# Scores of the first two head pairs as full fp32 products, with nine products on a constant ahead of them

## The chip, the cores and the metric

The kernel runs on one core of a Trainium2 chip. The metric is the device time of one execution in microseconds (us); lower is better. TensorE (PE) has two clock levels that matter here, 1.2 and 2.4 GHz; the profile gives the clock that was granted as a share of the full one.

## The reference, cut to what matters

A soft-capped attention is followed by two feed-forward stages. Only the attention is touched by the change:

```python
def _attn_ref(q, k, v, cap):               # q, k, v: (4, 12, 448, 64)
    scale = 1.0 / np.sqrt(q.shape[-1])
    scores = scale * np.matmul(q, k.transpose(0, 1, 3, 2))
    scores = cap * np.tanh(scores / cap)
    scores = scores - np.max(scores, axis=-1, keepdims=True)
    attn = np.exp(scores)
    attn = attn / (np.sum(attn, axis=-1, keepdims=True) + 1e-09)
    return np.matmul(attn, v).astype(np.float32)
# then, on the result reshaped to x (1792, 768):
#   r = relu(x @ w_in); x = (s * r * r + b) @ w_out      (d_ff = 2048)
#   soft mixture over 8 experts of 4 slots, with phi, w1, w2
```

`q` and `k` are drawn at standard deviation 6.4, so the scores are large. `w_in` and `w_out` arrive as float64.

## The kernel before, in words

**Pairs.** The 48 heads are taken as 24 pairs `p`, two heads on the two halves of the 128 partitions (64 each). Two pairs make a quad `Q`, 12 in all. For a pair, qT is 128 x 448 and kT 128 x 512: three full chunks of 128 keys, and a fourth in which the last 64 keys of both heads lie together.

**Loads.** `load_qk` issues the two loads of a pair on the SP queue. Pairs 0 and 1 go straight into the tiles `tmp` and `hh` (`c["early"]`, line 903), which lie idle at the start; later pairs into one buffer each of `q2` and `k2`, so that pair p + 1 can be loaded only when pair p has been split.

**Splitting.** `prep_pair` splits q and k into a high part, rounded to the reduced format fp32r, and the rest (`split`, lines 77 to 79): a cast (line 78) and a subtraction on DVE (line 79). The cast is on DVE for p < 6 except pair 1, whose casts are on ACT. The four results have three buffers each.

**Scores.** `scores` (line 114) makes one chunk of one pair: kh·qh + kh·ql + kl·qh, three reduced products for each of the two heads, on the two halves of the rows (line 125); the fourth chunk takes both heads in one product (line 122). Pairs of even number write their scores into one PSUM tile, the others into another. ACT then takes the tanh (lines 129, 131) and, when both pairs of a quad have a chunk, the exponential (line 194) of 4 x 448 columns.

**What runs beside it.** Products of the exponentials with v (line 229) and with a constant of ones (lines 212, 214) are full fp32 products on PE, 32 columns wide, four of them side by side. DVE adds the exponentials up (line 201) and takes the reciprocal (line 218). `attention` is a generator; `run` takes 52 steps of it (a little over three quads) before the feed-forward starts, and at every sixth step one unit of `convert`: it loads a slice of float64 `w_in` or `w_out` (line 351, 768 KB, two buffers), scales it on ACT (line 356) and puts the bits together on DVE (lines 361, 383, 387). `down` and `fold` (lines 435 to 448) reduce a w_out slice with `phi`, through `tmp` and `pw`, which is a part of `hh`. The result of quads 0 and 1 also goes through `hh` (line 241).

**What sets the order.** Everything before the branch on `cap` (line 939) is laid out as one block and everything inside as another. Within a block the tile framework's planner fixes each engine's order from the order of the program and from estimated durations; `high_priority` moves a few instructions ahead. At run time each engine takes its list strictly in order. The loads of pairs 0 and 1 and the constants stand before the branch, all else behind it.

**Behind the opening** come four feed-forward blocks (`hidden`, line 497; products at line 509) with the rest of the attention woven in, then a tail that streams the expert weights.

Of the kernel before, what the change touches and what calls it, by code (L numbers as in the profile page):

```python
# [7 lines left out]
F32 = mybir.dt.float32  # L8
# [6 lines left out]
PSUM = bass.MemoryType.PSUM  # L15
DRAM = bass.MemoryType.DRAM

P = 128
B, H, S, D = 4, 12, 448, 64
NP = H // 2  # L20
# [13 lines left out]
KF = S // P  # L34
# [5 lines left out]
STEPS = 8  # L40
LAST = 3
CASTS = NP
LEAD = 10
WIDE = 6
VISITS = (4, 7, 10, 13)
# [7 lines left out]
def load_qk(nc, io, p, q2, k2):  # L53

    nc.sync.dma_start(q2, io["qT"][p])
    nc.sync.dma_start(k2, io["kT"][p])


class Body:
# [43 lines left out]
        self.nc.sync.dma_start(self.v[p], self.io["v"][p])  # L103

    def prep_pair(self, p):
        if p >= B * NP:
            return
        q2, k2 = self.qk[p]
        t = [self.ap.tile([P, S if n[0] == "q" else KW], F32R, tag=n, bufs=2 if self.general else 3, name=n) for n in ("qh", "ql", "kh", "kl")]
        self.split(t[0], t[1], q2, p < CASTS and p != 1)  # L110
        self.split(t[2], t[3], k2, p < CASTS and p != 1)
        self.qk[p] = t

    def scores(self, p, c):

        nc = self.nc
        Q, j = divmod(p, 2)
        qh, ql, kh, kl = self.qk[p]
        sc = (self.ps2 if self.ps2 is not None and j else self.psa).tile([P, 2, 512], F32, tag="sc", bufs=1, name="sc")
        for n, (k, q) in enumerate(((kh, qh), (kh, ql), (kl, qh))):  # L120
            if c == KF:
                nc.tensor.matmul(sc[:, 0, :S], k[:, KF * P:], q, start=(n == 0), stop=(n == 2))
            for i in range(2) if c < KF else ():
                r = slice(64 * i, 64 * i + 64)
                nc.tensor.matmul(sc[:, i, :S], k[r, c * P:(c + 1) * P], q[r, :], start=(n == 0), stop=(n == 2))  # L125
        if j == 0:
            self.e.setdefault(Q, []).append(self.ap.tile([P, 4 if c < KF else 2, S], F32, tag="e", bufs=4 if self.general else 3, name="e"))
        if c < KF:
            nc.scalar.activation(self.e[Q][c][:, 2 * j:2 * j + 2, :], sc[:, :, :S], AF.Tanh, scale=self.c["tsc"])  # L129
        else:  # L130
            nc.scalar.activation(self.e[Q][c][:, j, :], sc[:, 0, :S], AF.Tanh, scale=self.c["tsc"])
        if c == NCH - 1:
            del self.qk[p]
# [614 lines left out]
    def block(self, bi, atn):  # L748
# [5 lines left out]
        for grp in range(4):  # L754
# [6 lines left out]
            for k in range(12):  # L761
                next(h)
                next(post, None)
                if bi < 2:
                    next(self.conv, None)
                while done < min(total, (12 * grp + k + 1) * total / (48 - LEAD)):
                    next(atn)
# [120 lines left out]
@with_exitstack  # L888
def tile_kernel(ctx: ExitStack, tc: tile.TileContext, io):
    nc = tc.nc  # L890
    cp = ctx.enter_context(tc.tile_pool(name="cp", bufs=1, side="left"))
    c = {}

    def t(name, shape, dt=F32):
        c[name] = cp.tile(shape, dt, name="c_" + name)
        return c[name]

    cap = t("cap", [P, 1])
    nc.sync.dma_start(cap, io["cap"].partition_broadcast(P))
    tmp, hh = t("tmp", [P, 1280]), t("hh", [P, 2, 512])  # L900
    acc, pw = hh[:, 0, :], hh[:, 1, :]
    c["acc"], c["pw"] = acc, pw.rearrange("p (a b) -> p a b", b=NS)
    c["early"] = [(tmp[:, :S], tmp[:, S:S + KW]), (acc[:, :S], pw[:, :KW])]
    for g in range(2):
        load_qk(nc, io, g, *c["early"][g])
    acap = t("acap", [P, 1])
    nc.vector.tensor_scalar(acap, cap, -1.0, None, op0=ALU.mult)
    nc.vector.tensor_max(acap, acap, cap)
    flag = t("flag", [1, 1], I32)
    nc.vector.tensor_scalar(flag, acap[0:1, :], CAP_FAST, None, op0=ALU.is_le)  # L910
    tsc = t("tsc", [P, 1])
    nc.vector.reciprocal(tsc, acap)
    nc.vector.tensor_scalar(tsc, tsc, SCALE, None, op0=ALU.mult)
    eps = t("eps", [P, 1])
    nc.scalar.activation(eps, acap, AF.Exp, scale=-1.0)
    nc.vector.tensor_scalar(eps, eps, EPS, None, op0=ALU.mult)
    nc.vector.memset(t("ones", [P, P]), 1.0)
    cst = t("cst", [P, 2, P])
    nc.gpsimd.dma_start(cst, io["cst"][:, 0:2, :])
    c["idn"], c["fold"] = cst[:, 0, :], cst[:, 1, :]  # L920
    misc = t("misc", [P, KC * NS + 64])
    c["phi"], c["hot"] = misc[:, :KC * NS].rearrange("p (a b) -> p a b", b=NS), misc[:, KC * NS:].rearrange("p (a b) -> p a b", b=32)
    nc.gpsimd.dma_start(c["hot"], io["hot"])
    for n in ("s", "b"):
        nc.gpsimd.dma_start(t(n, [P, 1]), io[n + "_"].partition_broadcast(P))
    t("selB", [P, 2, P], F32R)
    nc.gpsimd.dma_start(c["phi"], io["phi"])
    t("pbrow", [P, NS])
    t("pb", [P, 1])
    t("z", [P, 1])  # L930
    t("ct", [P, NT], F32R)
    f64 = io["w_in"].dtype == I64
    osc = []
    dp = ctx.enter_context(tc.tile_pool(name="dp", bufs=1, space=DRAM))
    wsc = [dp.tile([P, KC * P], F32, name=f"wsc{i}") for i in range(FC)]
    if f64:
        osc = [dp.tile([P, 4096], F32, name=f"osc{i}") for i in range(3)]
    rv = nc.values_load(flag, min_val=0, max_val=1, skip_runtime_bounds_check_because="a comparison writes 0 or 1")
    with tc.If(rv > 0) as br:
        Body(nc, tc, io, c, False, f64, wsc, osc).run()  # L940
    with br.Else():
        Body(nc, tc, io, c, True, f64, wsc, osc).run()
# [62 lines left out]
```

## Time and profile before

| what | us |
|---|---|
| runs of the kernel before | 654.86, 650.22, 654.69; median 654.69 |
| the profiled execution | 653.77 |
| its span, first to last instruction | 652.0 |
| PE busy | 597.1 |
| ACT busy | 408.8 |
| DVE busy | 341.4 |
| mean granted clock of PE | 0.982 |

The profile is of one execution. Busy times overlap between engines. PEld is the loading of weights into TensorE, which overlaps the products. An idle time in brackets, with an arrow, names what ended it. A count behind a row (x2) merges neighbours of one kind; a full fp32 product stands in the trace as two matmuls.

### The profile page before, as it was taken

The numbers are of one execution on the slowest core, as the hardware profiler recorded it, in microseconds if no ns is written. First come the engines' busy times: TensorE is split into PE (matmuls) and PEld (weight loads), VectorE is DVE, ScalarE is ACT, GpSimd is POOL, SyncE is SP. The second block draws the span as 40 slices with busy tenths as digits, with TensorE's granted clock in tenths as the row PEclk, the third lists the DMA queues.
The fourth block names the chain that finished last, engine by engine and source line by source line (L and its number), as shares of the span: only waits on it lengthen the run. The fifth ranks groups of instructions, "written<-read, shape, count | busy, mean of one in ns | idle before, by whom it ended". The sixth has DMA issues, their size and how long they took to land.

```text
span 652.0 us, 11248 instructions
## 1 busy us (share of the span) xinstructions
PE 597.1 (92%) x4564; PEld 392.7 (60%) x4564; DVE 341.4 (52%) x498; ACT 408.8 (63%) x690; POOL 4.1 (1%) x11
## 2 busy tenths in 40 slices
PE   5888999999999999999999999999999989998662
PEld 2333575656576656567587476768868874346451
DVE  4987789887973844574624826453332214112111
ACT  5988898888757957859569486865646551001010
POOL 1000000000000000000000000000000000000000
PEclk9998999999999999999999999999999998999996
DMA  7746567596676542041421321212977849999997
GB/s 276 248 130 212 168 210 272 209 303 220 222 249 241 186 134 98 25 138 50 130 81 49 114 72 42 73 49 86 381 279 270 332 160 376 418 418 419 417 406 264
DMA packets 41420, 137.39 MB, mean 211 GB/s; under 512 B 4353, under 2 KB 15889, under 8 KB 34449
## 3 DMA queue, kind: packets, MB, share of 16 engines
q1 hardware_dynamic: 41072, 136.07, 57.9%
q8 instruction: 38, 0.62, 0.4%
q0 software_dynamic: 288, 0.53, 0.2%
q14 instruction: 22, 0.17, 0.1%
HBM read 118.49 MB, written 18.09 MB: 209 GB/s over the span
## 4 chain that ended last, share of the span: by engine, by line
PE 59%; DMA 16%; DVE 12%; ACT 7%; issue 3%; SPq 0%; DVEq 0%
PE hp L509 27%; DMA wt<-in_w_dram 9%; PE U L229 8%; PE tp L524 4%; DMA raw<-in_w_outT_dram 3%; PE sc L153 3%; PE pt L603 2%; PE hps L824 2%; DVE es L201 2%; PE L L538 2%; DMA raw<-in_w_in_dram 2%; PE sc L125 1%; DMA k<-in_kT_dram 1%; PE tw L457 1%; DVE o L383 1%
## 5 line engine op out<-in xcount | busy, mean ns | idle before, releaser
L509 PE MATMUL hp<-x,ws 128*128 128x448 f32 x1152 | 270.1, 376 | 0.0
L509 PEld LDWEIGHTS hp<-x,ws 128*128 128x128 f32 x1152 | 207.0, 188 | 45.7 <-issue 32.6
L494 DVE TENSOR_TENSOR ws<-wr,ws 128x384 fp32r<-128x384 f32 x128 | 70.4, 552 | 118.5 <-ACT ws L493 115.8
L493 ACT CAST ws<-wr 128x384 fp32r<-128x384 f32 x128 | 66.4, 519 | 40.7 <-PE hp L509 40.0
L229 PE MATMUL U<-e,v 128*32 128x448 f32 (+1 forms) x672 | 76.8, 554 | 3.6 <-ACT e L194 2.6
L194 ACT ACTIVATE e<-e,c_acap 128x1792 f32<-128x1792 f32 (+1 forms) x42 | 71.1, 1693 | 0.4
L526 ACT COPY g<-tp 112x256 f32<-112x256 f32 x128 | 42.7, 383 | 17.7 <-PE tp L524 16.9
L229 PEld LDWEIGHTS U<-e,v 128*32 128x32 f32 (+1 forms) x672 | 20.6, 111 | 43.8 <-issue 36.2
L218 DVE RECIPROCAL rec<-rec 128x448 f32<-128x448 f32 x12 | 35.4, 2950 | 14.3 <-ACT rec L217 14.3
L524 PE MATMUL tp<-c_cst,r 128*112 128x128 f32 x256 | 39.1, 276 | 3.3 <-ACT g L526 1.6
L514 ACT ACTIVATE r<-hp 128x448 f32<-128x448 f32 x64 | 35.2, 550 | 9.7 <-PE hp L509 9.7
L156 ACT ACTIVATE e<-sc,c_tsc 128x896 f32<-128x896 f32 x36 | 35.7, 1026 | 4.8 <-PE sc L153 4.8
L857 ACT COPY wt<-op 128x512 f32<-128x512 f32 x12 | 7.0, 585 | 50.1 <-PE op L852 50.1
L515 ACT ACTIVATE r<-r 128x448 f32<-128x448 f32 x64 | 37.7, 589 | 0.6
L524 PEld LDWEIGHTS tp<-c_cst,r 128*112 128x112 f32 x256 | 29.0, 133 | 14.4 <-ACT g L526 4.3
L129 ACT ACTIVATE e<-sc,c_tsc 128x896 f32<-128x896 f32 x36 | 35.6, 1003 | 3.4 <-PE sc L125 3.2
L872 PE MATMUL so_ps<-wt,free 128*32 128x128 f32 x768 | 25.1, 275 | 11.8 <-DMA wt<-in_w_dram 11.8
L201 DVE TENSOR_TENSOR es<-e 128x1792 f32<-128x1792 f32 x12 | 24.3, 2022 | 11.1 <-ACT e L194 11.0
L872 PEld LDWEIGHTS so_ps<-wt,free 128*32 128x32 f32 x768 | 19.9, 109 | 15.6 <-DMA wt<-in_w_dram 13.5
L201 DVE TENSOR_TENSOR es<-es,e 128x1792 f32<-128x1792 f32 x12 | 24.3, 2021 | 7.7 <-ACT e L194 7.7
L125 PE MATMUL sc<-qh,kh 64*128 64x448 f32 x72 | 18.1, 486 | 11.1 <-DVE kh L78 6.4
L125 PEld LDWEIGHTS sc<-qh,kh 64*128 64x128 f32 x72 | 7.5, 198 | 24.3 <-issue 8.7
(168 smaller groups left out, 705.5 us busy)
## 6 DMA issues: line engine op xcount, KB each, us to landing
wt<-in_w_dram SPq DMA_DIRECT2D x48, 1024.0 KB, 15.3
wr<-wsc SPq DMA_DIRECT2D x48, 384.0 KB, 3.0
raw<-in_w_in_dram SPq DMA_DIRECT2D x16, 768.0 KB, 4.6
raw<-in_w_outT_dram SPq DMA_DIRECT2D x16, 768.0 KB, 4.9
wsc<-wr SPq DMA_DIRECT2D x16, 384.0 KB, 2.8
osc<-o SPq DMA_DIRECT2D x24, 256.0 KB, 2.2
wt<-osc SPq DMA_DIRECT2D x6, 1024.0 KB, 6.5
k<-in_kT_dram SPq DMA_DIRECT2D x22, 256.0 KB, 3.1
```

Of the source, the lines that this page charges most:

```text
L129: nc.scalar.activation(self.e[Q][c][:, 2 * j:2 * j + 2, :], sc[:, :, :S], AF.Tanh, scale=self.c["tsc"])
L156: nc.scalar.activation(self.e[Q][c][:, 2 * j:2 * j + 2, :], sc[j][:, :, :S], AF.Tanh, scale=self.c["tsc"])
L194: self.nc.scalar.activation(e, e, AF.Exp, scale=self.c["acap"])
L201: self.nc.vector.tensor_add(es, e[0] if c == 1 else es, e[c])
L229: nc.tensor.matmul(self.U[32 * i:32 * i + 32, h, :S], self.v[2 * Q + i // 2][self.rows(i, k), d:d + 32], self.chunk(4 * Q + i, k), start=( ...
L493: self.nc.scalar.copy(hi, u)
L494: self.nc.vector.tensor_sub(lo, u, hi.bitcast(F32))
L509: nc.tensor.matmul(hp[:, :S], ws[kc // 3][:, w, kc % 3, :], x[:, s, kc, :], start=(k == 0), stop=(k == 3 * KC - 1))
L515: self.mark = nc.scalar.activation(r2, r2, AF.Square).ins
L524: self.nc.tensor.transpose(tp[:CP, q * P:(q + 1) * P], r2[:, q * CP:(q + 1) * CP], self.c["idn"])
L526: self.nc.scalar.copy(self.g[q][:CP, :, fc * P:(fc + 1) * P], tp[:CP, 2 * q * P:2 * (q + 1) * P].rearrange("p (a b) -> p a b", b=P))
L872: nc.tensor.matmul(so_ps[32 * e:32 * e + 32, G, :], ht[G][:, f, 32 * e:32 * e + 32], w2[f // 4][:, f % 4, e, :], start=(f == 0), stop=(f = ...
```

## The change

Pairs 0 and 1 are no longer split. Their scores are one full fp32 product of k and q as they were loaded, per head and chunk, in place of three reduced products. Before them, and before the branch, nine full fp32 products of the constant `ones` with itself (128 x 128) are written to a PSUM tile that nobody reads; the memset of `ones` moves ahead of them in the program. All later pairs are as before.

```diff
+WHOLE = 2
@@ prep_pair
-        if p >= B * NP:
+        if p >= B * NP or p < WHOLE:
             return
         q2, k2 = self.qk[p]
...
-        self.split(t[0], t[1], q2, p < CASTS and p != 1)
-        self.split(t[2], t[3], k2, p < CASTS and p != 1)
+        self.split(t[0], t[1], q2, p < CASTS)
+        self.split(t[2], t[3], k2, p < CASTS)
         self.qk[p] = t
@@ scores
-        qh, ql, kh, kl = self.qk[p]
+        if p < WHOLE:
+            terms = [self.qk[p][::-1]]
+        else:
+            qh, ql, kh, kl = self.qk[p]
+            terms = (kh, qh), (kh, ql), (kl, qh)
+        last = len(terms) - 1
...
-        for n, (k, q) in enumerate(((kh, qh), (kh, ql), (kl, qh))):
+        for n, (k, q) in enumerate(terms):
             if c == KF:
-                nc.tensor.matmul(sc[:, 0, :S], k[:, KF * P:], q, start=(n == 0), stop=(n == 2))
+                nc.tensor.matmul(sc[:, 0, :S], k[:, KF * P:], q, start=(n == 0), stop=(n == last))
...
-                nc.tensor.matmul(sc[:, i, :S], k[r, c * P:(c + 1) * P], q[r, :], start=(n == 0), stop=(n == 2))
+                nc.tensor.matmul(sc[:, i, :S], k[r, c * P:(c + 1) * P], q[r, :], start=(n == 0), stop=(n == last))
@@ tile_kernel
     for g in range(2):
         load_qk(nc, io, g, *c["early"][g])
+    nc.vector.memset(t("ones", [P, P]), 1.0)
+    with tc.tile_pool(name="warm", bufs=1, space=PSUM) as warm:
+        w = warm.tile([P, P], F32, name="warm")
+        for _ in range(9):
+            nc.tensor.matmul(w, c["ones"], c["ones"], start=True, stop=True)
...
-    nc.vector.memset(t("ones", [P, P]), 1.0)
     cst = t("cst", [P, 2, P])
```

## Rows read from the trace of the kernel before

**Rows 1.** The page: busy tenths of 40 slices of the span.

```profile
PE   5888999999999999999999999999999989998662
DVE  4987789887973844574624826453332214112111
ACT  5988898888757957859569486865646551001010
DMA  7746567596676542041421321212977849999997
```

**Rows 2.** Windows: length, then busy us of each engine, granted clock, DMA.

```profile
core 0: us, PE busy (x) PEld busy (x) DVE busy (x) ACT busy (x) POOL busy (x), PEclk, DMA share, GB/s
...
5.00:9.40 4.40, 2.62 (x10) 1.50 (x12) 3.18 (x6) 2.07 (x3) 0.00 (x0) 1.00 0.94 336
...
6.30:14.50 8.20, 7.38 (x36) 3.82 (x39) 4.41 (x8) 6.46 (x7) 0.00 (x0) 1.00 1.02 391
...
16.00:44.00 28.00, 23.25 (x186) 10.07 (x186) 27.31 (x34) 25.45 (x29) 0.00 (x0) 1.00 0.53 174
...
52.30:56.30 4.00, 3.99 (x21) 1.42 (x21) 3.96 (x4) 3.51 (x3) 0.00 (x0) 0.57 0.57 216
...
60.00:540.00 480.00, 471.58 (x3005) 322.94 (x2998) 270.38 (x372) 347.55 (x616) 0.54 (x1) 1.00 0.49 169
```

**Rows 3.** The chain of waits in order of time: start us, us, what.

```profile
2.61 5.27 DMA c_hh<-in_kT_dram
...
10.10 1.02 ACT e L129
...
33.71 1.08 DVE c_hh L241
...
51.41 0.87 PE sc L125 x6
...
67.24 0.99 PE pp L439 x12
```

**Rows 4.** Timeline around 50 us: start us, us, what, idle before and its end.

```profile
49.57 0.89 ACT L356 ACTIVATE wr<-raw 128x768 f32<-128x768 f32 x1 [0.44 <-DMA raw<-in_w_in_dram]
50.36 1.90 ACT L129 ACTIVATE e<-sc,c_tsc 128x896 f32<-128x896 f32 x2
...
51.41 0.47 PE L125 MATMUL sc<-qh,kh 64*128 64x448 f32 x2 [2.93 <-ACT e L129]
```

**Rows 5.** Timeline of the first 15 us.

```profile
0.84 0.17 DVE L917 MEMSET c_ones<- 128x128 f32 x1 [0.84 <-PEq L995]
...
7.29 0.91 SPq L351 DMA_DIRECT2D raw<-in_w_in_dram  x2
...
14.65 0.56 DVE L361 TENSOR_SCALAR wr<-wr 128x768 int32<-128x768 int32 x1 [2.42 <-ACT wr L356]
```

**Rows 6.** The first two loads of the tile raw.

```profile
DMA to landing us min/median/max: 6.2/6.9/7.7
```

**Rows 7.** Line 356, 13 to 17 us: durations in ns, first and last start.

```profile
L356 ACT ACTIVATE wr<-raw x2: 890/902/913, 13.7 to 15.4; 128x768 f32<-128x768 f32 x2
```

**Rows 8.** Groups of ACT, 5 to 9.4 us: busy us, mean ns, idle before.

```profile
L78 ACT CAST kh<-c_hh 128x512 fp32r<-128x512 f32 x1 | 0.6, 618 | 0.8 <-DMA c_hh<-in_kT_dram 0.8
...
L78 ACT CAST qh<-c_hh 128x448 fp32r<-128x448 f32 x1 | 0.6, 565 | 2.1 <-DMA c_hh<-in_qT_dram 2.1
```

**Rows 9.** Timeline: the cast of pair 0's k.

```profile
5.78 0.43 DVE L78 CAST kh<-c_tmp 128x512 fp32r<-128x512 f32 x1
```

**Rows 10.** Timeline of PE and of its weight loads, from five places.

```profile
6.35 0.74 PE L125 MATMUL sc<-qh,kh 64*128 64x448 f32 x2 [6.35 <-DVE kh L78]
...
22.75 0.13 PEld L229 LDWEIGHTS U<-e,v 128*32 128x32 f32 x4 [0.25 <-issue]
...
261.31 1.02 PE L559 MATMUL lt_ps<-c_tmp,c_cst 128*128 128x448 f32 x2
...
536.86 1.77 PE L559 MATMUL lt_ps<-c_tmp,c_cst 128*128 128x448 f32 x2 [0.76 <-ACT c_tmp L556]
...
588.84 0.71 PE L881 MATMUL ss_ps<-c_tmp,sel 128*128 128x128 f32 x4 [0.61 <-DVE c_tmp L878]
```

## The prediction

> **What bounds the kernel now.** The page's slices come first, because the change sits in the first 22 us of 652. There PE is partly idle for the first three or four slices and then full to about slice 33, while DVE and ACT are nearly full early [rows 1]. The windows say it in microseconds: from 16 to 44 us DVE is busy 27.31 of 28 and ACT 25.45, PE 23.25, so DVE has only 0.69 us to spare; from 60 to 540 us PE is busy 471.6 of 480 [rows 2]. So the opening is paced by DVE and ACT, and what it saves or loses is handed on almost one to one by a full PE. In the last slices DMA is full too [rows 1]; those loads are issued behind work that itself shifts with PE, so I let the shift pass through.
>
> The chain of waits shows what the opening hangs on [rows 3]. Its first long piece is the landing of pair 1's k at 2.61 + 5.27 = 7.88 us; the first tanh of pair 1 starts at 10.10, and from 51.41 us PE is on it. Around 50 us there is a hole: ACT takes a conversion at 49.57 and only then a tanh at 50.36, PE stands still 2.93 us until 51.41 [rows 4], and then runs at a granted clock of 0.57 from 52.3 to 56.3 [rows 2], mostly the 1.2 GHz level. That hole will return below as a price.
>
> One more pair of facts decides my sum. The first two raw loads are issued from 7.29 us on, 0.91 us for both, so the second near 7.76 [rows 5]; they land after 6.2 and 7.7 us [rows 6], that is at 13.5 and 15.5. ACT converts them from 13.7 and 15.4 [rows 7]: the first conversion starts 0.2 us behind its data, the second with its data. DVE stood idle 2.42 us for the first one and starts at 14.65 [rows 5].
>
> **The change part by part.** *Removed.* The six DVE instructions in 5.00 to 9.40 us, 3.18 us busy, are just the casts and subtractions of pairs 0 and 1 [rows 2], and all go. So do ACT's two casts for pair 1, 0.62 + 0.57 = 1.18 us [rows 8]. On DVE I credit nothing: the time freed lies before the 2.42 us of idleness at 14.65, so it only lengthens it. The preparation of pair 2 comes next on DVE but waits for its own loads, which SP issues as before. For pair 3 fresh buffers replace those that pair 0 held; its loads still come after pair 2's preparation, so I take nothing.
>
> *Moved.* The memset of the constant is earlier in the program, but it already ran at 0.84 us, first on DVE [rows 5]: nothing. The raw tiles of pairs 0 and 1 now live until their last scores, about 21 us. Their next writers are the attention result at 33.71 us and what follows the first phi products of 67.24 us [rows 3], so no wait.
>
> *Added ahead.* Nine full fp32 products are 18 half products of 128 columns. The only such shape, line 881, does four in 0.71 us with 0.275 us of drain [rows 10], 0.145 us each at the upper clock; 18 make 2.6 us, or 5.2 at half clock. From about 1.05 us they end between 3.7 and 6.3. Pair 0's k is there at 5.78, when DVE began to cast it [rows 9], and PE did nothing before 6.35 [rows 10]. So they cost nothing; if the cover is short, at most 0.5 us of pair 0's first product, and pair 1's k is later still. Behind them on PE stands its load of the branch flag. Loads on SP don't wait for PE there.
>
> *Scores.* Three reduced products on the two halves of the rows took 0.20 us each at the upper clock: six in 0.87 us [rows 3], the first pair 0.47 [rows 4], so (0.87 - 0.47) / 2. That is 0.60 us per chunk and pair. A full product is two halves; in line 229, also fp32 with 448 columns, they follow each other by 0.13 + 0.25 = 0.38 us [rows 10], so 0.76 us, and with its drain line 559 takes 1.02 at the upper clock and 1.77 at the lower [rows 10]. Eight chunk products thus cost 8 x 0.16 = 1.3 us more of PE, if the two heads overlap on their halves of the rows. No row shows a 64-row fp32 product 128 columns wide. The nearest, the reduced products on the same tiles, overlap, and I take that; without overlap six chunks cost 6 x 0.76 = 4.6 us more.
>
> *On the path.* Pair 1's first tanh can start at 7.88 + 1.02 = 8.9 us instead of 10.10: 1.2 us sooner. At the lower clock it is 7.88 + 1.77 = 9.65, 0.45 sooner; at the lower clock and without overlap 1.5 us later again, 11.1, a loss of 1.0. I take the 1.2, since matmuls on a constant from 1 to about 5 us are like the dense stretch of 52.3 to 56.3, after which the clock was up. Then what is late next? The first conversion, bound to the landing at 13.5: sooner by 0.24 us at most; and the second, at 15.5, not at all. DVE's queue follows these and is then full to 44 us, so at most the 0.24 survives. Sum: 653.77 (the profiled execution, 652.0 span and 1.8 around it) - 0.24 = 653.5 us. That execution is 0.9 us under the median shown, 654.69, and inside the three runs, so I leave it.
>
> A rule weighed against this: the first scores at 6.35 us take 0.74 us for two, the time of the 0.57 stretch, not the 0.47 of 51.41 [rows 4, 10]; the granted-clock column reads 1.00 there all the same, and the durations decide. The Trainium skill ("TensorE: Matmul & The Clock Gate", section "Terms") prices throttled time at that time x (1 - K/N), half of it here. By that rule the warmed clock would be worth about half of PE's 7.38 busy us between 6.3 and 14.5 [rows 2], 3.7 us; by the landings it is worth nothing beyond the 0.24. It is rival A.
>
> **The rivals.**
> A. PE's clock carries: the products up to 14.5 us run twice as fast, and the opening shortens by 7.38 / 2 = 3.7 us, 650.1. For it: PE does wait in short gaps there and ACT follows it. Against: ACT and DVE are the fuller engines, and the landings hold both. Chance 0.13.
> B. The order changes. Each engine's order is laid out ahead by estimated durations; 3 us less of DVE early can turn ACT's order near 50 us, so that the hole goes: 2.9 us idle and half of the 4 us at the lower level, 4.9 in all, 648.6. For it: tanh and conversion stand there in an order that hurts. Against: nothing but luck makes the order better. Chance 0.12.
> C. Slower: the same reordering opens a second such hole in the opening, a tanh queued behind a conversion whose raw data is in flight, with PE idle about 3 us and the clock fallen: 653.5 + 4.9 = 658.4. It decides when ACT reaches the conversion more than about 1 us ahead of the landing; ACT now comes 1.2 us sooner to the one at 13.5, so the first wait is there, but PE then has other products. Chance 0.14.
> D. The two heads don't overlap in full fp32: up to 4.6 us of PE, of which the 1.2 gained covers some; 653.8 + 3.4 = 657 at worst, near 654.5 more likely. Chance 0.08.
> E. The clock isn't up when pair 0 starts, so the products do not do what they are there for: the tanh gains 0.45 instead of 1.2, and the landing still holds: 653.5 to 653.8, the same time. Chance 0.05.
>
> **How the numbers follow.** The forecast itself has 0.48, and its own range is 651.5 to 655, which is the 1.2 us of ACT, the 0.7 us that DVE has left and the spread of the three runs. The range for 8 in 10 adds most of A and D and part of B and C: 649.0 to 657.5. One per cent, about what a measurement of this kernel can tell from no change, is 6.5 us: only B with A on top (0.05) or C with D or worse (0.04) reach it; 0.91 is left for no change.
>
> **What would show it.** In the changed profile: nine products on the constant from about 1 us; first scores at 5.8 to 6.3 with about 1 us for a pair of heads; tanh of pair 1 near 8.9; the first conversion at 13.5, waiting for raw, the second at 15.4 to 15.5; DVE full from about 14.4; the PE hole near 50 us still there, about 0.2 us sooner. A first conversion at 12.5, or PE full before 55 us, would refute the sum. Wrong by over 5 us would mean that the order of ACT or DVE between 16 and 70 us changed, seen as a different sequence of conversions and tanhs.

## The result, and the profile after

The changed kernel took 655.94 us (median of 12 executions, 653.17 to 663.45), the kernel before on the same chip 653.46 (12, 648.49 to 655.69). The ratio is 1.0053, 95% interval 1.0027 to 1.0079: a loss of about 3.5 us by the ratio (2.5 by the medians) where 0.24 us of gain was forecast. 655.94 lies inside the range for 8 in 10, 649.0 to 657.5, but above the forecast's own range of 651.5 to 655, and on the far side of no change.

The execution that was profiled took 653.17 us, the shortest of its twelve, and the one before 653.77, so the two totals don't show the loss. The streaming tail, from the last feed-forward product to the end, took 119.0 us before and 116.0 in the change, and 115.4 to 119.3 over the twenty profiled executions of this document. A mark ahead of the tail leaves that out: the first feed-forward product (line 509, now 515) starts at 68.2 us before and at 71.0 after, the last at 533.0 and 535.3. The loss is in the opening and is carried through, 2.8 and 2.3 us.

The slices of the page, as [rows 1]:

```profile
PE   6888999999999999999999999999999998997662
DVE  2988679887965764492632835455342214112211
ACT  4989888889866957959569577766645662101010
...
DMA  7636458588576553041431311221968839999998
```

DVE falls from 4 to 2 in the first slice, which is the removed splitting; from the fourth slice on it has 8, 6 and 7 where it had 7, 7 and 8. Work was removed, and what is left lies later. The windows, with the columns of [rows 2]:

```profile
5.00:9.40 4.40, 2.79 (x14) 1.10 (x12) 0.00 (x0) 1.45 (x2) 0.00 (x0) 1.00 0.93 336
16.00:44.00 28.00, 23.14 (x162) 8.60 (x162) 25.99 (x32) 26.98 (x29) 0.00 (x0) 0.88 0.48 165
18.00:26.00 8.00, 7.20 (x42) 1.77 (x40) 8.00 (x9) 7.60 (x9) 0.00 (x0) 0.79 0.74 249
34.00:42.00 8.00, 7.04 (x47) 2.68 (x46) 6.64 (x8) 7.47 (x8) 0.00 (x0) 0.79 0.19 70
52.30:56.30 4.00, 2.64 (x16) 1.94 (x20) 3.96 (x5) 3.97 (x5) 0.00 (x0) 0.61 0.91 323
60.00:540.00 480.00, 471.71 (x3018) 322.45 (x3011) 271.25 (x373) 348.82 (x617) 0.54 (x1) 1.00 0.49 168
```

DVE did 3.18 us from 5.0 to 9.4 before and does nothing there now. From 16 to 44 us it was busy for 27.31 of 28 us and now for 25.99: 1.3 us more in which DVE, the engine that set the pace, stands idle. The granted clock of that stretch fell from 1.00 to 0.88. From 60 to 540 us nothing changed, 471.7 us of PE against 471.6.

The timeline of the changed kernel, rows of PE, ACT, DVE and SP's queue in order of time, up to the feed-forward:

```profile
1.06 4.21 PE L916 MATMUL warm<-c_ones 128*128 128x128 f32 x18 [1.06 <-DVE c_ones L912]
5.84 1.02 PE L131 MATMUL sc<-c_tmp 64*128 64x448 f32 x4 [0.57 <-DMA c_tmp<-in_kT_dram]
8.96 1.01 ACT L135 ACTIVATE e<-sc,c_tsc 128x896 f32<-128x896 f32 x1 [0.99 <-PE sc L131]
11.01 0.33 SPq L56 DMA_DIRECT2D q<-in_qT_dram  x1
13.97 0.90 ACT L362 ACTIVATE wr<-raw 128x768 f32<-128x768 f32 x1 [1.29 <-DMA raw<-in_w_in_dram]
14.90 0.56 DVE L367 TENSOR_SCALAR wr<-wr 128x768 int32<-128x768 int32 x1 [2.86 <-ACT wr L362]
15.90 0.89 ACT L362 ACTIVATE wr<-raw 128x768 f32<-128x768 f32 x1 [1.03 <-DMA raw<-in_w_in_dram]
16.45 0.39 DVE L79 CAST qh<-q 128x448 fp32r<-128x448 f32 x1 [0.99 <-DMA q<-in_qT_dram]
16.69 0.99 ACT L135 ACTIVATE e<-sc,c_tsc 128x896 f32<-128x896 f32 x1
16.76 0.95 DVE L389 SCALAR_TENSOR_TENSOR wr<-raw,wr 128x768 int32<-128x768 int32 x1
17.63 0.55 DVE L367 TENSOR_SCALAR wr<-wr 128x768 int32<-128x768 int32 x1
17.74 1.02 PE L131 MATMUL sc<-c_hh 64*128 64x448 f32 x4 [3.24 <-ACT e L135]
18.10 0.95 DVE L393 SCALAR_TENSOR_TENSOR wr<-raw,wr 128x768 int32<-128x768 int32 x1
19.50 0.38 SPq L357 DMA_DIRECT2D raw<-in_w_outT_dram  x1
19.56 3.12 PE L235 MATMUL U<-e,v 128*32 128x448 f32 x16 [0.80 <-ACT e L200]
22.61 1.02 PE L128 MATMUL sc<-c_tmp 128*128 128x448 f32 x2
33.50 0.47 PE L131 MATMUL sc<-qh,kh 64*128 64x448 f32 x2 [1.36 <-ACT e L135]
36.22 4.83 PE L235 MATMUL U<-e,v 128*32 128x448 f32 x32 [0.94 <-DVE c_hh L247]
53.66 0.74 PE L131 MATMUL sc<-qh,kh 64*128 64x448 f32 x2 [2.75 <-ACT e L135]
```

The same places in the timeline of the kernel before, so far as they don't stand above:

```profile
11.03 0.33 SPq L55 DMA_DIRECT2D q<-in_qT_dram  x1
13.73 0.89 ACT L356 ACTIVATE wr<-raw 128x768 f32<-128x768 f32 x1
14.52 0.99 ACT L129 ACTIVATE e<-sc,c_tsc 128x896 f32<-128x896 f32 x1
15.24 0.96 DVE L383 SCALAR_TENSOR_TENSOR wr<-raw,wr 128x768 int32<-128x768 int32 x1
16.24 0.96 DVE L387 SCALAR_TENSOR_TENSOR wr<-raw,wr 128x768 int32<-128x768 int32 x1
17.65 0.38 SPq L351 DMA_DIRECT2D raw<-in_w_outT_dram  x1
18.08 1.71 PE L229 MATMUL U<-e,v 128*32 128x448 f32 x16 [1.12 <-ACT e L194]
21.38 0.39 DVE L78 CAST qh<-q 128x448 fp32r<-128x448 f32 x1
34.84 3.21 PE L229 MATMUL U<-e,v 128*32 128x448 f32 x32 [1.05 <-DVE c_hh L241]
```

Read them as two lists that were reordered. **ACT:** before, conversion (13.73), tanh of pair 1's second chunk (14.52), conversion (15.44). After, both conversions stand ahead of that tanh, the second waits 1.03 us for its raw data, the tanh starts at 16.69 instead of 14.52, and PE waits 3.24 us for it. **DVE:** before, the cast of pair 3's q stood at 21.38, behind the bit assembly of both raw slices. After, it stands inside that assembly and waits 0.99 us for its own load, issued at 11.01 as before. The rest of the first slice's assembly (now line 389) starts behind it, at 16.76 instead of 15.24, and the second slice's first step (line 367) has moved in between, to 17.63. Only the last step (line 393), at 18.10 instead of 16.24, frees the raw buffer, so SP's load of the next slice goes out at 19.50 instead of 17.65. Of the 1.86 us at that last step the later first conversion is 0.25 (14.90 against 14.65), the cast with its wait 1.27 and the step that moved in 0.34.

Then PE is at the lower clock twice (a granted clock of 0.79 from 18 to 26 and from 34 to 42 us, 1.00 in both before): sixteen matmuls on v take 3.12 us instead of 1.71, thirty-two take 4.83 instead of 3.21. The hole near 50 us, of [rows 4], is still there with 2.75 us.

### The profile page after: what moved, and what is told of

It is laid out like the page before. It is cut to its first block, busy times and chain, and to the rows that moved or that the text cites. A ratio compares the mean times of both kernels' runs of the same rounds, so it can differ in the third digit from the quotient of the medians.

```text
span 651.3 us, 11245 instructions
## 1 busy us (share of the span) xinstructions
PE 599.0 (92%) x4568; PEld 393.5 (60%) x4568; DVE 338.3 (52%) x492; ACT 408.4 (63%) x688; POOL 4.1 (1%) x11
## 4 chain that ended last, share of the span: by engine, by line
PE 38%; DMA 12%; ACT 3%; DVE 1%; issue 1%; SPq 0%
PE hp L515 21%; DMA wt<-in_w_dram 12%; PE U L235 4%; PE tp L530 3%; PE sc L159 2%; PE pt L609 2%; PE L L544 2%; PE si_ps L809 1%; PE sc L149 1%; ACT e L162 1%; PE Sm L218 1%; ACT e L200 0%; PE xp L819 0%; PE lt_ps L565 0%; ACT g L532 0%
## 5 line engine op out<-in xcount | busy, mean ns | idle before, releaser
L500 DVE TENSOR_TENSOR ws<-wr,ws 128x384 fp32r<-128x384 f32 x128 | 70.4, 552 | 118.6 <-ACT ws L499 115.9
L235 PE MATMUL U<-e,v 128*32 128x448 f32 (+1 forms) x672 | 79.7, 575 | 2.5 <-ACT e L200 1.6
L224 DVE RECIPROCAL rec<-rec 128x448 f32<-128x448 f32 x12 | 35.4, 2951 | 14.5 <-ACT rec L223 14.5
L830 PE MATMUL hps<-wt,free 128*32 128x512 f32 x192 | 21.0, 593 | 0.0
L131 PE MATMUL sc<-qh,kh 64*128 64x448 f32 x60 | 14.6, 467 | 5.2 <-ACT e L135 5.0
```

The source lines that it names most:

```text
L235: nc.tensor.matmul(self.U[32 * i:32 * i + 32, h, :S], self.v[2 * Q + i // 2][self.rows(i, k), d:d + 32], self.chunk(4 * Q + i, k), start=( ...
L500: self.nc.vector.tensor_sub(lo, u, hi.bitcast(F32))
```

## The experiments

The 18 runs below were made in five groups on a chip, each beside the kernel before. "First product" is the start of the first feed-forward product and "clock" the granted clock from 34 to 42 us, both from the one profiled execution. Ratios are against the kernel before of the same group.

| kernel | median us | ratio [95% interval] | first product | clock |
|---|---|---|---|---|
| before | 653.46 | | 68.2 | 1.00 |
| the change | 655.94 | 1.0053 [1.0027, 1.0079] | 71.0 | 0.79 |
| 1 change without the nine products | 654.52 | 1.0026 [0.9998, 1.0054] | 71.4 | 0.79 |
| 2 before with the nine products | 654.0 | 1.001 [0.9982, 1.0038] | 68.1 | 1.00 |
| 3 change, second conversion held behind the tanh (ACT) | 653.69 | 1.0026 [0.9995, 1.0057] | 70.7 | 1.00 |
| 4 before, tanh held behind the second conversion (ACT) | 651.39 | 1.0005 [0.9973, 1.0038] | 68.7 | 0.79 |
| 5 change, pair 3's split held behind the assembly (DVE) | 655.21 | 1.0028 [1.0002, 1.0055] | 70.4 | 0.80 |
| 6 change, both held, as in 3 and 5 | 652.02 | 0.9998 [0.9972, 1.0024] | 69.1 | 1.00 |
| 7 before, pair 0 in buffers of its own | 653.24 | 1.0024 [0.999, 1.0057] | 70.2 | 0.79 |
| 8 as 6, without the nine products | 653.28 | 1.0002 [0.9976, 1.0029] | 70.7 | 1.00 |
| 9 the change again | 655.12 | 1.0047 [1.002, 1.0073] | 72.2 | 0.59 |
| 10 as 6, again | 653.9 | 1.0021 [0.9997, 1.0045] | 69.5 | 1.00 |
| 11 as 6, three raw buffers | 649.59 | 0.9979 [0.9949, 1.0008] | 66.8 | 1.00 |
| 12 before, three raw buffers | 651.81 | 1.0002 [0.9969, 1.0036] | 70.3 | 0.59 |
| 13 change, nine products in PE's wait | 653.43 | 0.9992 [0.9963, 1.0021] | 67.3 | 1.00 |
| 14 as 13, six more in the first wait | 654.1 | 1.0011 [0.9985, 1.0037] | 70.7 | 1.00 |
| 15 as 7, again | 654.89 | 0.9998 [0.9967, 1.0029] | 72.5 | 0.61 |
| 16 as 11, again | 651.42 | 0.9958 [0.993, 0.9985] | 66.7 | 1.00 |
| 17 change, two products in PE's wait | 654.29 | 1.0052 [1.0019, 1.0085] | 72.1 | 0.79 |
| 18 change, five products in PE's wait | 652.43 | 1.0011 [0.998, 1.0042] | 67.2 | 1.00 |

**Is it the products on the constant?** Run 1 is the change without them, run 2 the kernel before with them.

```diff
-    with tc.tile_pool(name="warm", bufs=1, space=PSUM) as warm:
-        w = warm.tile([P, P], F32, name="warm")
-        for _ in range(9):
-            nc.tensor.matmul(w, c["ones"], c["ones"], start=True, stop=True)
```

> The changed kernel without the nine products on the constant; every other engine's order is that of the changed kernel, line for line. Theory O (order): the loss is the order that the planner laid out for ACT once pairs 0 and 1 are not split, with the second conversion ahead of pair 1's tanh of chunk 1; PE then waits some 3 us near 15 to 18 us. It expects no change against the changed kernel: 1.003 to 1.008 of the kernel before, the first feed-forward product at 70 to 72 us. Rival T (the clock): the products on the constant warm PE too early and the clock falls in the waits that follow; without them the time goes back to 0.998 to 1.002. First scores at the lower clock either way: about 1.7 us for a pair of heads in place of 1.02.

> The kernel before with the nine products on the constant ahead of it and the splits as they were; the order of every other engine is that of the kernel before, line for line. Theory O: same as before, 0.998 to 1.002, the first feed-forward product at 68 us within 0.5. Rival T: 1.003 to 1.008. Rival A of the prediction (PE's clock carries the opening): 0.994 or less, the first feed-forward product 3 us sooner.

Without them the mark stays late (71.4); with them alone it is where it was (68.1), at 1.001. The order of ACT, DVE and SP is that of the parent in both. The products neither cost nor give anything that can be resolved: the interval of run 2 leaves out a gain over 0.18%, 1.2 us.

What they do for the clock differs between executions of one kernel. In the profiled execution of the change the first scores took 1.02 us (at 5.84, above). In run 9, which is the change again, they took 1.86, and pair 1's tanh started at 9.70 instead of 8.96:

```profile
5.82 1.86 PE L131 MATMUL sc<-c_tmp 64*128 64x448 f32 x4 [0.55 <-DMA c_tmp<-in_kT_dram]
9.70 1.01 ACT L135 ACTIVATE e<-sc,c_tsc 128x896 f32<-128x896 f32 x1 [0.91 <-PE sc L131]
```

Of the twelve profiled executions with the nine products ahead of full fp32 scores, three show 1.02 us (the change, 11 and 16) and nine 1.86 or 1.87, the time of runs 1 and 8, which lack the products. The granted clock from 5.0 to 9.4 us reads 1.00 in the change and in run 9 alike, so at this place the durations tell and that column does not. In run 2's profiled execution the first pair of products took 0.48 us instead of 0.74, but those from 8.54 to 11.65 us again 0.56 to 0.74. So run 2 bounds what the nine products are worth, and not what a clock would be worth that stays up to 14.5 us.

**Which order?** Two edits put the order back by hand, with the planner's means of issuing one instruction behind another. The first holds the second conversion behind the tanh (ACT); the second holds the split of pair 3 behind the second slice's bit assembly (DVE). Run 4 does the reverse of the first in the kernel before.

```diff
+            if (p, c) == (1, 1):
+                for f in self.held:
+                    with self.tc.issue_after(t.ins):
+                        f()
...
+            if ahead and n == 0:
+                self.held = [lambda: scale(1), lambda: first(1)]
```

```diff
+        with self.tc.issue_after(self.bits[1]) if p == 3 and not self.general else nullcontext():
+            self.split(t[0], t[1], q2, p < CASTS)
+            self.split(t[2], t[3], k2, p < CASTS)
```

> The changed kernel with one thing set by hand: ACT's second conversion is held behind pair 1's tanh of chunk 1, as it stood in the kernel before. Theory O: PE's wait near 15 to 18 us shrinks from 3.2 us to about 1, the first feed-forward product comes at 67.5 to 69 us and the time is 0.997 to 1.002 of the kernel before. Rival F (the full fp32 scores themselves cost it): 1.004 to 1.008 still, the product at 70 to 72.

> The kernel before, splits and all, with that one order turned round: pair 1's tanh of chunk 1 is held behind ACT's second conversion. Theory O: the loss appears without the change, 1.002 to 1.007, the first feed-forward product at 69.5 to 72 us, PE waiting 1.5 to 3 us more between 14 and 20 us. Rival F: 0.998 to 1.002.

> The changed kernel with one thing set by hand: DVE's split of pair 3 is held behind the second raw unit's bit assembly, where it stood in the kernel before. Theory D: in the changed kernel nothing holds pair 3's buffers, so its cast is planned ahead of the bit assembly, waits there for its own load, and the next raw load goes out 1 to 2 us late; DVE and ACT are full behind it, so the time is not won back. It expects the raw load back at 17.5 to 18.5 us, the first feed-forward product at 68 to 69.2 us (71.0 in the changed kernel, 68.2 before) and 0.998 to 1.002. If ACT's order is needed as well (theory D and O): 69.3 to 71, 1.001 to 1.005.

> Both orders set by hand: e5 and e3 together. From pair 2 on DVE's list is then that of the kernel before, line for line; only the splits of pairs 0 and 1 are missing, the scores of these are full fp32, and the nine products stand ahead. Theories D and D with O: the first feed-forward product at 67 to 68.3 us and 0.996 to 1.001, the landing of raw at 13.5 us still holding the gain to a few tenths. Rival F (the full fp32 scores cost it by themselves): 70 us or later and 1.003 or more.

Run 3 takes the 3.24 us hole away, yet the mark is still late by 2.5 us and the interval reaches from nothing to 0.57%. The timeline of run 3 shows a second hole:

```profile
24.98 0.89 ACT L367 ACTIVATE o<-raw 128x768 f32<-128x768 f32 x1 [1.90 <-DMA raw<-in_w_outT_dram]
25.91 0.56 DVE L372 TENSOR_SCALAR o<-o 128x768 int32<-128x768 int32 x1 [1.34 <-ACT o L367]
...
27.12 0.47 PE L132 MATMUL sc<-qh,kl 64*128 64x448 f32 x2 [2.49 <-DVE kl L81]
```

ACT waits 1.90 us for the next raw slice, DVE 1.34 us for ACT, and PE 2.49 us for a rest of k that stands behind DVE's wait. That slice's load went out at 18.60 in this run against 17.65 before: the DVE order makes its late load by itself. The load also took 6.4 us to land, 4.5 before, which is the larger part of this wait. Run 5 puts pair 3's split back behind the assembly and keeps ACT's order and a first hole (2.25 us); its load still goes out late, at 18.51, since the second slice's first step stays within the first one's assembly, and the ratio stays at 1.0028. Run 4 has the ACT order without the DVE order and loses nothing that can be resolved; it is not quite clean, since the split of pair 3 moved too (to 19.42, still behind the bit assembly) and the load after next went out sooner, at 19.96 instead of 21.92. So in the kernel before the ACT order was not seen to cost anything by itself. In the changed kernel it does cost: runs 5 and 6 differ by the hold on ACT and by what the planner makes of it, and in one group 655.21 us stands against 652.02 (0.1 to 0.5% by drawing the single times anew). Neither repair by itself brings the ratio clearly back. With both repaired, run 6 stands at 0.9998, and from the preparation of pair 2 on DVE's list is that of before, line for line; so are ACT's and SP's. Its timeline:

```profile
9.79 1.01 ACT L138 ACTIVATE e<-sc,c_tsc 128x896 f32<-128x896 f32 x1 [0.93 <-PE sc L134]
...
13.42 0.94 ACT L369 ACTIVATE wr<-raw 128x768 f32<-128x768 f32 x1
14.24 1.01 ACT L138 ACTIVATE e<-sc,c_tsc 128x896 f32<-128x896 f32 x1
...
17.39 0.38 SPq L364 DMA_DIRECT2D raw<-in_w_outT_dram  x1
...
34.55 3.21 PE L242 MATMUL U<-e,v 128*32 128x448 f32 x32 [1.01 <-DVE c_hh L254]
...
51.45 0.74 PE L134 MATMUL sc<-qh,kh 64*128 64x448 f32 x2 [3.30 <-ACT e L138]
```

The tanh is at 14.24, 0.28 us sooner than before, the load at 17.39, 0.26 sooner, and the matmuls on v at 34.55, 0.29 sooner. That has the size of the 0.24 us that was forecast, but not its reason. The first raw load landed after 5.8 us here (6.2 before, 6.6 in run 10, 6.7 in the change), so the first conversion, at 13.42, waited for nothing; it is 0.31 us sooner because pair 1's tanh, behind scores that took 1.83 us, came at 9.79 instead of 10.10. In runs 8 and 10 it waits 0.71 and 0.24 us for its data and starts at 14.20 and 13.73, no sooner than before. Nor is the lead kept. Near 50 us ACT waits 1.21 us for a raw slice, 0.44 before, PE's hole is 3.30 us instead of the 2.93 of [rows 4] (4.71 and 3.42 in runs 8 and 10), and the scores behind it take 0.74 us instead of 0.47; the mark is 0.9 us late.

> e6 without the nine products on the constant, every other engine's order unchanged line for line. If the clock is hidden behind the landings as the prediction said: the first feed-forward product within 0.4 us of e6's and the ratio within 0.002 of it. If the warmed clock is worth something once the order is right (rival A in small): 0.5 to 1.5 us later.

> The changed kernel as it is, beside e10 on one chip. Theory (both orders): 1.002 to 1.006 of the kernel before, the first feed-forward product 2 to 3.5 us behind the 68.2 of the kernel before.

> e6 once more beside it. Theory (both orders): 0.996 to 1.001 and faster than e9 by 0.2 to 0.5 per cent; the first feed-forward product at 67.5 to 69.2 us. If what separated e6 from the changed kernel was chance: within 0.1 per cent of e9.

Run 8 is run 6 without the nine products: 1.0002 beside 0.9998. All its loads behind those of pairs 0 and 1 went out some 0.5 us late, the raw ones at 7.78 instead of 7.29, which is a part of its late mark. Runs 9 and 10 repeat the change and run 6: 1.0047 and 1.0021. Run 9 tells where the loss sits when the raw data lands sooner (7.2 us for the second load instead of 8.2): the first hole is only 1.46 us and the clock stays at 1.00 from 18 to 26 us, and still the mark is at 72.2. Its windows, then the second of them in the kernel before, and one row of run 9's timeline:

```profile
18.00:26.00 8.00, 7.00 (x52) 2.75 (x56) 8.00 (x11) 8.00 (x11) 0.00 (x0) 1.00 0.87 296
34.00:42.00 8.00, 6.65 (x37) 2.30 (x38) 5.63 (x7) 6.00 (x6) 0.00 (x0) 0.59 0.01 4
```

```profile
34.00:42.00 8.00, 6.80 (x60) 2.90 (x62) 8.00 (x10) 7.83 (x8) 0.00 (x0) 1.00 0.16 43
```

```profile
35.35 5.75 PE L235 MATMUL U<-e,v 128*32 128x448 f32 x32 [1.72 <-DVE c_hh L247]
```

The thirty-two matmuls on v take 5.75 us instead of 3.21, and from 34 to 42 us DVE has work for 5.63 of 8 us and ACT for 6.00, where before they had 8.00 and 7.83. So in this execution the hole at 17.74 is not the main loss; the stretch from 34 us on is. Which of the two orders that stretch goes with stays open: its clock is 1.00 in run 3 and 0.79 and 0.61 in runs 7 and 15, which have the moved cast of pair 3 without the moved conversion, and 0.79 and 0.80 in runs 4 and 5, which have the conversion without the cast. Taken together, the four runs whose DVE and ACT orders are the change's (the change, 1, 9 and 17) have ratios of 1.0026 to 1.0053, mean 1.0045; the three with both restored (6, 8 and 10) 0.9998 to 1.0021, mean 1.0007. The difference, 0.0038 or 2.5 us, is what the order costs; drawing the single times of each run anew puts it between 0.2 and 0.5%. The marks agree: 71.0 to 72.2 us in those four, 68.1 to 70.7 in the five executions with the lists of before (before, 2, 6, 8 and 10), though these five scatter by 2.6 us themselves. Whether 0.07% is left beside the order these runs don't tell.

**Is it the freed buffers?** In the kernel before, pair 0's split results get buffers of their own, so that pair 3 no longer has to wait for them. Nothing else is touched.

```diff
-tag=n, bufs=2 if self.general else 3, name=n)
+tag=n + "0" * (p == 0 and not self.general), bufs=1 if p == 0 and not self.general else 2 if self.general else 3, name=n)
```

> The kernel before, splits and reduced products and all, with one change: pair 0's split results have buffers of their own, so that pair 3 finds its three free, as in the changed kernel. The planner then moves pair 3's cast ahead of the bit assembly on DVE. Theory D: the loss appears without the change, the first feed-forward product at 69.3 to 71 us, 1.002 to 1.006. Rival F: 68.2 within 0.5, 0.998 to 1.002.

> e7 once more: the kernel before with buffers of their own for pair 0's split results. Theory D: 1.002 to 1.005 again, the first feed-forward product 1.5 to 3 us behind that of the kernel before, the granted clock in 34 to 42 us below 1.00. If e7 was chance: 0.998 to 1.001 and 68.2 within 0.5.

In the trace the cast of pair 3's q moves from 21.38 to 16.15, in between the bit assembly, and the next raw load from 17.65 to 18.32. So the freed buffer is what lets the planner move it: that step is shown. The mark comes at 70.2 and 72.5 and the clock falls to 0.79 and 0.61. The time, 1.0024 and 0.9998 with intervals 0.6% wide, does not resolve a loss. That the DVE order alone costs what the change costs is therefore not shown.

**Is it the clock?** Products on the constant are put into PE's wait near 32 us, behind the scores of pair 3's second chunk; in run 14 six more behind those of pair 0's third. Nothing reads their results.

```diff
+FILL = {(3, 1): 9}
...
+            with self.tc.issue_after(mm.ins):
+                b = self.bank("fill")
+                for _ in range(fill):
+                    nc.tensor.matmul(b[:, :P], self.c["ones"], self.c["ones"], start=True, stop=True)
```

> The changed kernel with nine more products on the constant, placed on PE behind the scores of pair 3's chunk 1, where it waits 1.4 us and then 0.9 to 1.7 us. Theory C (the clock): the granted clock in 34 to 42 us is 1.00 in place of 0.59 to 0.79, the 32 products on v there take 3.2 us in place of 4.8 to 5.8, the first feed-forward product comes 1 to 2 us sooner than 71.0 to 72.2 us and the time is 1.000 to 1.003. Theory L (the conversions' lateness itself): clock 1.00 but the first feed-forward product still at 70.5 or later, 1.004 to 1.007.

> e13 with six more products behind pair 0's chunk 2, in PE's wait of 1.5 to 3.2 us before 18 us. Theory C: as e13 or up to 1 us better, since the clock does not fall near 20 us in any execution either. Theory L: as the changed kernel or worse by what the products hold up, 1.004 to 1.008.

> The change with two more full products on the constant behind the scores of pair 3, chunk 1, where PE waits near 32 and 35 us. Every engine's list is that of the change, these two products apart, so unlike the run with nine of them nothing else moves. Two products are only some 0.3 to 0.6 us of work in a wait of 2.3. If the fallen clock near 36 us is what costs, and two products hold it: granted clock above 0.95 from 34 to 42 us, the 32 products on v in 3.2 to 3.6 us, first feed-forward product near 68.5, ratio about 1.001. If they don't hold it: clock about 0.8 and product near 71 as in the change, ratio 1.003 to 1.005, and the clock stays untried alone. If the waits themselves cost and not the clock: clock up, product still near 71, ratio 1.003 to 1.005.

> The same place with five products. SP's list is now that of the run with nine, in which the load of the next raw slice stands some 6 us sooner, and DVE's and ACT's lists are nearly it. If that run was mended by the moved load and not by the clock: first feed-forward product near 67.5 and ratio about 0.999, whatever the clock from 34 to 42 us. If by the clock: the same only with a granted clock above 0.95; with a clock of about 0.8 the product near 70 and ratio 1.003 or more. Clock up and time mended would leave both open.

With nine and with five products the clock stays up, the mark comes at 67.3 and 67.2, and the loss isn't seen (0.9992, 1.0011). But the added work also changed the planner's lists: a load of the next raw slice moved from 46.63 to 40.85 and 40.51 us. With two products only those two are added to any list, and the clock falls all the same; a window of run 17 and one row of its timeline:

```profile
34.00:42.00 8.00, 5.08 (x33) 1.55 (x34) 7.23 (x7) 6.80 (x6) 0.00 (x0) 0.79 0.24 92
```

```profile
36.92 4.91 PE L242 MATMUL U<-e,v 128*32 128x448 f32 x32 [3.16 <-DVE c_hh L254]
```

It repeats the loss, 1.0052, and the late mark, 72.1. But it is no test of the same wait: in the profiled execution a raw slice came late, ACT waited 2.33 us for it, and PE stood 3.16 us ahead of the thirty-two matmuls instead of 0.94. Run 14 has the clock up from 14 to 64 us and a load moved to 41.82, and the mark is still late (70.7) at a ratio of 1.0011. In runs 4, 7, 12 and 15 the clock falls and no loss is resolved. So the fallen clock goes along with the new order, but how much of the 2.5 us is the clock and how much the waits and late loads behind it stays open: no run kept the clock up on the change's own lists.

**A version that is faster.** If late raw loads hurt, a third raw buffer should help. It also puts a third load at the start and changes the planner's lists.

```diff
-        self.raws = 2
+        self.raws = 3
```

> e6 with a third buffer for raw slices, so that a load goes out one unit earlier. If the landings of raw hold the opening, as the prediction's sum says: ACT's conversions no longer wait for them after the second, the first feed-forward product at 64.5 to 67 us and 0.990 to 0.996. If DVE and ACT are the bound without the landings: 67.5 to 69 and 0.997 to 1.002.

> The kernel before with the third raw buffer: what the landings are worth without the change. Landings: 65 to 67.5 us for the first feed-forward product, 0.991 to 0.997. DVE and ACT: 67.5 to 69 us, 0.997 to 1.002. The difference to e11 is what the change is worth when raw doesn't hold it: 0.5 to 1.2 us by the tanh of pair 1.

> e11 once more: the change with both orders set by hand and a third raw buffer. If its lead is real: 0.995 to 0.999 of the kernel before, the first feed-forward product at 66 to 68 us. If chance: 0.999 to 1.002.

On top of run 6 it gives 0.9979 and 0.9958, the second with an interval that ends at 0.9985, and marks of 66.8 and 66.7; in the kernel before it gives 1.0002. The version beats the kernel before by some 0.3%, 2 us, and the change by 655.12 - 649.59 = 5.5 us in medians of one group. With three buffers alone the mark is at 70.3 and the clock at 0.59, so the buffer does not do it by itself. Runs 11 and 12 are also the cleanest pair for the edit itself: their lists of ACT, DVE and SP are the same but for the casts and subtractions that the change removes. In one group 649.59 us stand against 651.81, so with raw loads a slice ahead and the order kept the edit gains some 0.3% (0.0 to 0.6 by drawing the single times anew; run 12 was not repeated), where with two buffers nothing is left of it.

## Why the prediction was wrong

**Right.** The nine products ran from 1.06 to 5.27 us, inside 3.7 to 6.3, and cost nothing. The first scores came at 5.84, right behind the landing of k. Two heads took 1.02 us in four half products, as the 128-row form does, so they overlap (rival D falls), and in this execution the clock was up. The tanh of pair 1 started at 8.96 against 8.9. The first conversion waited for its data, and the second too, at 13.97 and 15.90; both 0.4 to 0.5 us later than the sum had put them, 13.5 and 15.5, since the loads took longer in this execution. The hole near 50 us stayed (B falls). With both orders held the opening of run 6 ran 0.26 to 0.29 us sooner, the size of the 0.24, but by luck: there the landing held nothing, and by 68 us the lead was gone.

**Wrong, the first step.** "For pair 3 fresh buffers replace those that pair 0 held; its loads still come after pair 2's preparation, so I take nothing." The loads did stay, 11.01 against 11.03. What moved was the split: pair 0's buffers had held it behind the bit assembly in DVE's list, and without them it went ahead, to wait 0.99 us for a load in flight. The step asked when the data comes and not where the instruction would stand. The wait is small; what is queued behind it frees a raw buffer, and the next load goes out 1.85 us later, 19.50 against 17.65, 1.27 of it by the cast and its wait.

**Wrong, the second step.** Rival C named the mechanism and its place, a tanh queued behind a conversion whose raw data is in flight, and had 0.14. Its own condition, ACT more than 1 us ahead of the landing, was met (1.29 and 1.03 us of waiting). It was set aside because "PE then has other products". PE had none: it waited 3.24 us. Its price of 4.9 us was 2.9 of hole and 2 of lower clock. The profiled execution has a hole of 3.24, and 1.41 + 1.62 us more for the forty-eight matmuls on v; 2.8 us of this reach the first feed-forward product, and by the repeated times 2.5 to 3.5 us the end. But C saw only ACT's half: with ACT's order put right (run 3) the ratio is still 1.0026, and in run 9, with a hole of 1.46, the mark is later still, the larger part of it by 34 to 42 us, a stretch of which C says nothing.

**A chance mis-sized.** Rival E, the clock not up when pair 0 starts, had 0.05, because products from 1 to 5 us were taken to be like the dense stretch from 52.3 to 56.3. It was the common case, nine of twelve profiled executions; the tanh of pair 1 is then at 9.70 (run 9), near the 9.65 that the prediction gives for it. Its price, none, was not contradicted: without the products at all run 1 stands at 1.0026 beside the change's 1.0053 and 1.0047.

**The rule that was weighed.** Rival A took the early clock to be worth 3.7 us by the Trainium skill's price for throttled time ("TensorE: Matmul & The Clock Gate", "Terms"); in the profiled execution of the change it came to nothing. Its products up to 14.5 us have the durations of the upper level and the tanh of pair 1 is 1.14 us sooner, and then ACT waits 1.29 and 1.03 us for raw data. The landings hold the opening there, as the sum had it. Run 2 can't settle the rule, since its clock did not stay up.

**The chances.** Within 1% had 0.91, and 0.5% is within it; but the likeliest case was put at no change and the order at luck, better or worse. A part of the order could have been read from the code: pair 0's buffers held pair 3's split back, and the change gives them up. A list of what stood behind that split on DVE would have raised C. Why the planner moved the second conversion ahead of the tanh was not isolated.

## What to carry to other kernels

When an edit frees a buffer early in a kernel whose order is planned, ask which instruction that buffer held back, where it will now stand in its engine's list, and whether its own data is there by then; a wait of one microsecond is paid by all that stands behind it. Here removing 3.2 us of DVE's work was worth nothing that could be resolved while two raw buffers set the loads, some 0.3% with three, and it invited reordering: hold the old order by hand first, and then measure the edit. For changes of this size take a mark ahead of the noisy tail, and still let the repeated times decide, since the mark of one execution misled in runs 7, 8, 12 and 15.

## What the runs showed of the hardware

The granted clock did not follow the length of PE's waits alone. In run 16 two waits of 1.38 and 1.61 us just ahead of the thirty-two matmuls on v left the clock at 1.00; in the change 1.36 and 0.94 us at the same place went with 0.79. The timeline of run 16:

```profile
31.73 0.47 PE L134 MATMUL sc<-qh,kh 64*128 64x448 f32 x2 [1.38 <-ACT e L138]
...
35.12 3.21 PE L242 MATMUL U<-e,v 128*32 128x448 f32 x32 [1.61 <-DVE c_hh L254]
```

And a full fp32 product of 64 rows by 128 columns, of which no row of before told, costs two heads together 1.02 us, just what line 128 takes for one 128-row product in the same kernel (1.02 us at 22.61, in the timeline of the change above).

Nine full products from 1.06 to 5.27 us, some 0.6 us ahead of the first scores, did not settle the clock of those scores: 1.02 us in three executions and 1.86 or 1.87 in nine, with runs of one kernel among both (the change and run 9).
